# Retention and feed-forward on one core: work moved between places of an instruction order written by hand

## The chip, the core and the metric

The kernel runs on one core of a Trainium2 chip. The metric is the device time of one execution in microseconds (us). Before the change it is 857.37 us, the median of three runs (856.86 to 859.24). Everything below about the kernel before comes from one profiled execution of it. The engines are PE (TensorE matmul), PEld (TensorE weight load), DVE (VectorE), ACT (ScalarE), POOL (GpSimd) and SP (SyncE, which here only issues transfers, DMAs).

## The reference, cut to what matters

Retention (a linear attention with a decay for each head) over 8 batches, 8 heads, 576 positions and 64 channels, and a feed-forward block on its output, all in float32:

```
scores = q @ k.T / 8 ;  ret = scores * gamma_h ** (i - j) for i >= j, else 0
x   = (ret @ v), heads side by side        # 4608 tokens x 512
h   = x @ w_in                             # 512 x 2048
g   = h - tanh(h)
out = g @ w_out                            # 2048 x 512
```

## The kernel before, in words

The 576 positions are cut into nine chunks n = 0 to 8 of 64 positions; a chunk with its 8 batches is a block of 512 tokens. A float32 product is made of three products of rounded words: a tile is split into a high word (an ACT copy that rounds) and a low word (a DVE subtraction), and high by high, high by low and low by high are summed in PSUM. The 2048 middle channels are 16 tiles f of 128, in eight pairs j.

From chunk 3 on two chunks are multiplied with `w_in` at a time by a scheme with seven products in place of eight (`product`, `product_c`; products 0 to 6 of a pair j). It needs seven variants of x (`xv[0]` to `xv[6]`, each a tile of high and one of low words) and seven of each pair of `w_in`, which were written to memory before (`wvar`). What comes out are the four blocks c11, c12, c21 and c22 of h; for each a tanh runs on ACT (L1078, L1277) and a subtraction on POOL (`away`, which also stores g to `spill`) or on DVE (L1105, L1111, L1318).

- `stage_a(3)`: chunks 3 and 4, pairs j = 0 to 7. Chunk 3's g is split into words at once (`split`) and multiplied with `w_out` by `mm2_pair`, one pair behind (L1117); chunk 4's is stored. The block c21 of a pair is finished by `rest` (L1110): for j = 0 it waits in `pending` and runs inside pair 1, for the others it runs at the pair's own end. The sums that make the variants of `w_out` for later are made in `out_sums(j - 1)` (six DVE additions, L1147, two ACT roundings, L1150), called inside pair j behind c22 (L1093); their low words (L1154) and stores follow.
- `stage_b(4, ...)`: chunk 4's g is fetched and multiplied with `w_out` (`mm2`, L572, f = 0 to 15). Before each even f a "stretch" of small 64 x 64 matmuls (L344) computes retention for a later chunk (`stretch`, L935); it reads the running `state`, the masked scores (L356) and v scaled by ACT (`scale_v`, L301, called through `prep_turn(m, 1)`). `out_sums(7)` runs at f = 3, its store at f = 5 (L1528 to L1532).
- `stage_c(5, ...)`: chunks 5 and 6, now with a stretch in front of each of the eight pairs (p = j = 0 to 7). All g goes to `spill`. In the last pair the variants of x are made again for the next stage: `renew(na, k)` is called as soon as product k has been issued (its ACT rounding, L1242), and the low words (L1243) go into the list `lows`, from which `low()` takes one at fixed places.
- `stage_c(7, ...)`: chunks 7 and 8, pairs in falling order (p counts up, j down). It has no stretches; `ahead_c(p, k)` behind product k loads the variants of `w_out` for the second half (`load_second`; the lists `ahead_at` and `SPLITS` say when), splits some of them (`split_second`, L1353 and L1356), fetches the stored g (`fetch_group`) and starts its sums (`side_pieces`).
- The second half multiplies g of chunks 5 to 8 with `w_out` by the same scheme: eight groups of seven products q (`second_product`, L1462 and L1466), in the order `ORDER2` = B11, T1, T2, B22, T3, B21, T4, summed in three PSUM banks by `CHAIN`. In front of each q stand `side(q + 3)` and, for q = 1 to 4, one more `split_second`.

The order of the instructions is that of the program: `in_order` ties each engine's instructions to their order in the code. A buffer is named by its tag, and a tile waits until the one that had its buffer has been read or stored. All loads and stores named here are issued on SP's queue, in program order as well; one that must wait holds up those behind it.

Three buffers take part. The tag "g" has three buffers, which c22, c12 and c21 of every pair share. In `stage_c` the PSUM bank of x (products 0 and 5) is "own" in the last stage and "o0" in the one before, for every pair. The words of `w_out`'s variants go into places that the program has done with: B21's last two tiles into "wo1" and "wo0", which hold words of `w_in` for pair 0, the last to be computed, and the tiles of T3 and T4 into places of `xv`.

Of the kernel before, what the change touches and what calls it, by code (L numbers as in the profile page):

```python
# [19 lines left out]
P = 128  # L20
# [72 lines left out]
def retention_ffn(ctx: ExitStack, tc: tile.TileContext, ins, out, spill, wvar, ovar, ofull):  # L93
# [971 lines left out]
    def stage_a(na):  # L1065

        nb, pending, sums_too = na + 1, [], na + 2 == LATE
        u4 = work[:, 1]
        for j in range(NPAIR):
            u2 = work[:, 3 * (j % 2)]  # L1070
            x, y = [psp.tile([P, BLK], F32, tag=t, bufs=1, name=f"p{t}{na}_{j}") for t in ("new" if j else "o0", "own")]
            z, v = [psp.tile([P, BLK], F32, tag="h", bufs=2, name=f"p{t}{na}_{j}") for t in "zv"]
            f1, f2 = 2 * j, 2 * j + 1
            c22, c12, c21 = [pool.tile([P, BLK], F32, tag="g", bufs=3, name=f"c{t}_{na}_{j}") for t in (22, 12, 21)]

            def tanh(c):
                th = pool.tile([P, BLK], F32, tag="cv", bufs=4, name=f"th{na}_{j}")
                nc.scalar.activation(th, c, AF.Tanh)  # L1078
                return th

            def away(c, f):
                nc.gpsimd.tensor_tensor(c, c, tanh(c), op=ALU.subtract)  # L1082
                nc.sync.dma_start(spill[nb, f], c)

            product(0, x)
            product(1, y)
            nc.scalar.copy(u2, x)
            nc.vector.tensor_tensor(u2, y, u2, op=ALU.add)
            product(2, z)
            nc.vector.tensor_tensor(u4, z, u2, op=ALU.add)  # L1090
            product(3, v)
            nc.vector.tensor_tensor(c22, v, u4, op=ALU.add)
            low_sums = out_sums(j - 1) if sums_too and j > 0 else None  # L1093
            while pending:
                pending.pop()()
            y = psp.tile([P, BLK], F32, tag="own", bufs=1, name=f"py{na}_{j}")
            product(4, y)
            away(c22, f2)
            nc.vector.tensor_tensor(c12, y, u4, op=ALU.add)
            if low_sums:  # L1100
                low_sums()
            product(5, x, False)
            away(c12, f1)
            g11 = tanh(x)
            nc.vector.tensor_tensor(g11, x, g11, op=ALU.subtract)  # L1105
            product(6, v, False)
            split(na, f1, g11, False)
            nc.vector.tensor_tensor(c21, v, u2, op=ALU.add)

            def rest(f=f2, c=c21, tanh=tanh):  # L1110
                nc.vector.tensor_tensor(c, c, tanh(c), op=ALU.subtract)  # L1111
                split(na, f, c, True)

            if j == 0:
                pending.append(rest)
            else:
                mm2_pair(na, j - 1)  # L1117
                rest()
        if sums_too:
            load_turn(held, 1)  # L1120
            load_turn(held + 1, 1)
        for f in range(3):
            fetch(nb, f)
        if sums_too:
            prep_turn(held, 1)
        mm2_pair(na, NPAIR - 1)
        for f in range(2):
            split(nb, f, fetched.pop((nb, f)), False)

    def out_sums(j):  # L1130

        f1, f2 = [wout[2 * j + u].bitcast(F32) for u in range(2)]
        if j == NPAIR - 1:
            both = pool.tile([P, 2, DM], F32, tag="xl0", bufs=1, name=f"r{j}")
            r1, r2 = [both[:, u] for u in range(2)]
            wides = pool.tile([P, 2, 2, 2, Q], F32R, tag="xh0", bufs=1, name=f"to{j}")
            wides = [wides[:, u] for u in range(2)]
        else:
            r1, r2 = [pool.tile([P, DM], F32, tag="cv", bufs=4, name=f"r{j}_{u}") for u in range(2)]
            wides = [pool.tile([P, 2, 2, Q], F32R, tag=t, bufs=1, name=f"to{j}_{t}") for t in ("vr", "one")]  # L1140
        t1, t2, t3, t4 = [w[:, u, 1].bitcast(F32) for w in wides for u in range(2)]
        for to, a, b, op in (
            (r1, f1[:, 0], f1[:, 1], ALU.add), (r2, f2[:, 0], f2[:, 1], ALU.add),
            (t1, r1[:, Q:], r1[:, :Q], ALU.subtract), (t2, r2[:, Q:], t1, ALU.subtract),
            (t3, r2[:, Q:], r1[:, Q:], ALU.subtract), (t4, r2[:, :Q], t2, ALU.subtract),
        ):
            nc.vector.tensor_tensor(to, a, b, op=op)  # L1147
        words = [(T2, wides[0][:, 1:2]), (T3, wides[1])]
        for _, w in words:
            nc.scalar.copy(w[:, :, 0], w[:, :, 1].bitcast(F32))  # L1150

        def low_sums(store=True):
            for _, w in words:
                nc.vector.tensor_tensor(w[:, :, 1], w[:, :, 1].bitcast(F32), w[:, :, 0].bitcast(F32), op=ALU.subtract)  # L1154
            if store:
                store_sums()

        def store_sums():
            nc.sync.dma_start(ofull[:, B11, j], r1[:, :Q])
            nc.sync.dma_start(ofull[:, B21 : B22 + 1, j], r2.rearrange("p (k m) -> p k m", k=2))  # L1160
            nc.sync.dma_start(ofull[:, T1, j], t1)
            for at, w in words:
                n = w.shape[1]
                nc.sync.dma_start(ovar[:, at - T2 : at - T2 + n, j], w.bitcast(F32).rearrange("p v s m -> p v (s m)"))

        return (low_sums, store_sums) if j == NPAIR - 1 else low_sums

    raw, tslots, sources = {}, {}, {}
    RAWS = [(j, v) for j in range(NPAIR) for v in (0, 5, 6)]
# [75 lines left out]
    def stage_c(na, m0, lows):  # L1245

        nb, last_ = na + 1, na + 2 == NC
        if not last_:
            new_sources(na)
        homes_ = ("own", "new", "h", "h") if last_ else ("o0", "o1", "o2", "o3")  # L1250
        for p in range(NPAIR):
            j = NPAIR - 1 - p if last_ else p
            sums_of = None if last_ else attend_c(m0 + j)
            if sums_of and j == NPAIR - 1:
                sums_of()
# [4 lines left out]
                for w, t in zip("xyzv", homes_)  # L1260
            ]
            f1, f2 = 2 * j, 2 * j + 1
            c22, c12, c21 = [pool.tile([P, BLK], F32, tag="g", bufs=3, name=f"c{t}_{na}_{j}") for t in (22, 12, 21)]

            def done(k):
                if last_:
                    ahead_c(p, k)
                elif j == NPAIR - 1:
                    lows.append(renew(na, k))

            def low():
                if lows:
                    lows.pop(0)()
# [9 lines left out]

            product_c(na, j, 0, x)
            nc.scalar.copy(u2, x)
            done(0)
            if not last_:
                load_turn(m0 + j + 3, 0)
# [2 lines left out]
            low()  # L1291
            done(1)
            if not last_:
                prep_turn(m0 + j + 1, 1)
                load_turn(m0 + j + 2, 1)
                load_raws(6 + j)
            product_c(na, j, 2, z)
# [19 lines left out]
            g11 = tanh(x)  # L1317
            nc.vector.tensor_tensor(g11, x, g11, op=ALU.subtract)  # L1318
            nc.sync.dma_start(spill[na, f1], g11)
            low()  # L1320
            done(5)
            product_c(na, j, 6, v, False)
            nc.vector.tensor_tensor(c21, v, u2, op=ALU.add)
            away(na, c21, f2)
            done(6)

    second_w = {}

    def load_second(at, i):

        tags = {
            T1: ["wo12", "wo13", "wo14", "wo15"], B11: ["wo11", "wo10", "wo9", "wo8"],
            B22: ["wo7", "wo6", "wo5", "wo4"], B21: ["wo3", "wo2", "wo1", "wo0"],
        }
        homes_ = [place_of(f) for f in range(NF) if f not in (0, 2)]
        tags |= {T2: [place_of(0), place_of(2), "qk", "qk"], T3: homes_[6:10], T4: homes_[10:14]}
        where, bufs = (pool, 2) if tags[at][i] == "qk" else (const, 1)
        w = where.tile([P, 2, 2, Q], F32R, tag=tags[at][i], bufs=bufs, name=f"w2_{at}_{i}")
        if at < T2:
            nc.sync.dma_start(w[:, :, 1].bitcast(F32), ofull[:, at, 2 * i : 2 * i + 2])  # L1340
            unsplit.append(w)
        else:
            nc.sync.dma_start(w.bitcast(F32).rearrange("p j s m -> p j (s m)"), ovar[:, at - T2, 2 * i : 2 * i + 2])
        for u in range(2):
            second_w[at, 2 * i + u] = w[:, u]
# [15 lines left out]
    def fetch_group(k):  # L1361
# [16 lines left out]
        (0, 0): [(T1, 0), (T1, 1)], (0, 4): [(T1, 2), (T1, 3)], (1, 0): [(B11, 0)], (2, 0): [(B11, 1), (B11, 2)],  # L1378
        (3, 0): [(B11, 3)], (4, 0): [(B22, 0), (B22, 1)], (4, 4): [(T2, 0)], (5, 0): [(B22, 2), (T2, 1)],
        (5, 4): [(T2, 2)], (6, 0): [(B22, 3), (B21, 0)], (6, 4): [(T2, 3)], (7, 0): [(B21, 1)],  # L1380
        (7, 4): [(T3, i) for i in range(4)], (7, 6): [(B21, 2), (B21, 3)],
    }
    SPLITS = [
        (1, 1), (1, 3), (1, 5), (2, 1), (2, 3), (3, 1), (3, 3), (4, 1), (5, 1), (5, 3), (6, 1), (6, 5), (7, 1),
# [123 lines left out]
    def stage_b(n, m0):  # L1508

        fetch(n, 3)  # L1510
        for f in range(NF):
# [14 lines left out]
                load_slot(2)  # L1526
            if n == LATE - 1:
                if f == 3:  # L1528
                    low_sums, store_sums = out_sums(NPAIR - 1)
                    low_sums(False)  # L1530
                if f == 5:
                    store_sums()  # L1532
                if f in (11, 13):
                    load_sums(LATE, (f - 11) // 2)
                if f > 3 and f % 2 == 0:
                    load_raws(f // 2 - 2)
# [125 lines left out]
```

## Time and profile before

| what | value |
|---|---|
| median of three runs | 857.37 us |
| the profiled execution's own time | 857.09 us |
| its span, first to last instruction | 855.3 us |
| PE busy | 829.9 us, 97% of the span |
| DVE, ACT, POOL busy | 70%, 48%, 11% of the span |
| mean granted TensorE clock | 0.993 of full speed |
| transfers | 204.11 MB, 239 GB/s on average |

Where the stages lie, in us from the start of the span: `stage_a(3)` from about 317 to 443, `stage_b(4)` from there to 505, `stage_c(5)` to 602, `stage_c(7)` to 687, the second half from there to the end. PE is busy nearly throughout; the place to read is the little time in which it isn't, and what ended each of those pauses. "Issue" as a releaser means that the profile shows nothing that the engine waited for.

### The profile page before, as it was taken

What the parts mean: (1) busy time and instruction counts of PE and PEld (TensorE: products, weight loads), DVE (VectorE), ACT (ScalarE), POOL (GpSimd) and SP (SyncE); (2) the same over time, 40 slices, a digit from 0 to 9 for tenths busy, and PEclk for the clock granted to TensorE, in tenths of its full rate; (3) what the DMA queues carried; (4) which work ended last, traced back from release to release, by engine and by line L of the source; (5) the groups of instructions that cost most, each with busy time, mean ns of one, the idle gap of its engine ahead of it and who ended that gap; (6) DMA issues with size and microseconds to landing.
All of it is one profiled execution on the core that took longest, in us unless ns stands there. A gap on an engine that the chain in (4) does not pass through costs nothing.

```text
span 855.3 us, 19226 instructions
## 1 busy us (share of the span) xinstructions
PE 829.9 (97%) x7829; PEld 687.0 (80%) x7830; DVE 596.8 (70%) x947; ACT 408.9 (48%) x772; POOL 97.8 (11%) x79
## 2 busy tenths in 40 slices
PE   8999999999999999999989998999899888999997
PEld 6888888888888887888878887888677677888886
DVE  6999877777667665665648665456654768888884
ACT  5987755444245533333244544335443454444542
POOL 0000101010000002111110003233333320000000
PEclk9999999999999999999999999999999999999999
DMA  9968978884777677667378989784579897444411
GB/s 354 360 234 277 346 218 255 243 288 166 229 282 259 206 261 248 227 254 269 137 238 289 328 273 367 257 311 151 196 248 331 284 307 250 152 129 123 123 36 39
DMA packets 94520, 204.11 MB, mean 239 GB/s; under 512 B 9184, under 2 KB 35168, under 8 KB 90976
## 3 DMA queue, kind: packets, MB, share of 16 engines
q1 hardware_dynamic: 93984, 202.10, 69.2%
q8 instruction: 61, 1.00, 0.5%
q10 hardware_dynamic: 448, 0.79, 0.3%
q14 instruction: 27, 0.22, 0.1%
HBM read 135.22 MB, written 67.63 MB: 237 GB/s over the span
## 4 chain that ended last, share of the span: by engine, by line
PE 84%; DMA 5%; issue 4%; DVE 3%; ACT 2%; POOL 1%; SPq 0%; POOLq 0%; DVEq 0%; ACTq 0%
PE o L572 20%; PE h L514 15%; PE b L1462 11%; PE b L1466 6%; PE o L1058 5%; PE px L1195 3%; PE s L344 3%; PE pv L1195 3%; PE new L344 2%; PE pv L1027 2%; PE pnew L1027 2%; PE py L1195 2%; PE pz L1195 2%; PE pw L1195 2%; DMA spill_dram<-c 2%
## 5 line engine op out<-in xcount | busy, mean ns | idle before, releaser
L1462 PE MATMUL b<-w,s 128*128 128x512 f32 x336 | 118.7, 400 | 2.2 <-DVE w L1353 2.2
L572 PE MATMUL o<-wo,gh 128*128 128x512 f32 x432 | 110.8, 394 | 0.2 <-DMA vr<-in_qkv_dram 0.2
L514 PE MATMUL h<-xh,wi 128*128 128x512 f32 x380 | 96.6, 392 | 0.2 <-ACT wi L148 0.2
L572 PEld LDWEIGHTS o<-wo,gh 128*128 128x128 f32 x432 | 79.9, 188 | 18.1 <-DMA vr<-in_qkv_dram 0.6
L1466 PE MATMUL b<-w,s 128*128 128x256 f32 x336 | 87.7, 282 | 0.0
L1281 POOL TENSOR_TENSOR c<-c,th 128x512 f32<-128x512 f32 x48 | 63.4, 1325 | 197.0 <-ACT th L1277 97.7
L514 PEld LDWEIGHTS h<-xh,wi 128*128 128x128 f32 x380 | 70.6, 188 | 15.7 <-ACT wi L148 0.7
L1462 PEld LDWEIGHTS b<-w,s 128*128 128x128 f32 x336 | 61.9, 190 | 14.3 <-DVE w L1353 2.5
L1277 ACT ACTIVATE th<-c 128x512 f32<-128x512 f32 x48 | 30.1, 632 | 85.9 <-DVE c L1306 51.8
L1466 PEld LDWEIGHTS b<-w,s 128*128 128x128 f32 x336 | 64.1, 191 | 3.7
L572 PE MATMUL o<-wo,gl 128*128 128x512 f32 x216 | 59.7, 389 | 0.0
L344 PE MATMUL own<-qk,state 64*64 64x64 f32 x888 | 54.5, 221 | 0.0
L344 PE MATMUL own<-qk,vr 64*64 64x64 f32 x888 | 53.2, 218 | 0.0
L514 PE MATMUL h<-xl,wi 128*128 128x512 f32 x192 | 51.8, 390 | 0.0
L572 PEld LDWEIGHTS o<-wo,gl 128*128 128x128 f32 x216 | 40.5, 188 | 8.4
L1195 PE MATMUL px<-xhv,raw 128*128 128x512 f32 x128 | 41.3, 404 | 4.6 <-DVE th L1318 4.0
L344 PEld LDWEIGHTS own<-qk,vr 64*64 64x64 f32 x888 | 44.4, 135 | 0.0
L344 PEld LDWEIGHTS own<-qk,state 64*64 64x64 f32 x888 | 44.3, 134 | 0.0
L1082 POOL TENSOR_TENSOR c<-c,th 128x512 f32<-128x512 f32 x16 | 21.3, 1345 | 197.4 <-ACT th L1078 184.4
L514 PEld LDWEIGHTS h<-xl,wi 128*128 128x128 f32 x192 | 36.0, 188 | 7.6
L301 ACT ACTIVATE vr<-vr,vtab 128x128 f32<-128x128 f32 x100 | 32.1, 396 | 17.8 <-DMA vr<-in_qkv_dram 17.8
L344 PEld LDWEIGHTS s<-qk 64*64 64x64 f32 x928 | 29.3, 135 | 9.2 <-issue 5.3
(331 smaller groups left out, 1913.1 us busy)
## 6 DMA issues: line engine op xcount, KB each, us to landing
spill_dram<-c SPq DMA_DIRECT2D x64, 256.0 KB, 3.7
s<-spill_dram SPq DMA_DIRECT2D x62, 256.0 KB, 4.0
qk<-in_qkv_dram SPq DMA_DIRECT2D x29, 512.0 KB, 4.8
vr<-in_qkv_dram SPq DMA_DIRECT2D x29, 512.0 KB, 5.0
wt<-wvar_dram SPq DMA_DIRECT2D x14, 1024.0 KB, 6.8
ws<-wvar_dram SPq DMA_DIRECT2D x13, 1024.0 KB, 5.2
spill_dram<-g SPq DMA_DIRECT2D x36, 256.0 KB, 3.5
rwi<-in_w_in_dram SPq DMA_DIRECT2D x16, 512.0 KB, 6.3
```

The source lines that it names most:

```text
L301: nc.scalar.activation(v[:, :, i], v[:, :, i], AF.Copy, scale=vtab[:, n, i : i + 1])
L344: nc.tensor.matmul(out_, w, x, start=start, stop=stop)
L514: nc.tensor.matmul(hp, win[f][:, cc // 2, a, cc % 2 * P : (cc % 2 + 1) * P], x[:, cc, :], start=(k == 0), stop=(k == 3 * NCC - 1))
L572: nc.tensor.matmul(ops[n][t], g[:, t * P : (t + 1) * P], wout[f_][:, a, :], start=(f_ == first and k == 0), stop=(f_ == final and k == 2),)
L1027: nc.tensor.matmul(into, w[:, a, k], x[:, k], start=start and i == 0, stop=i == len(terms) - 1, skip_group_check=not start,)
L1058: nc.tensor.matmul(ops[n][t], g[:, t * P : (t + 1) * P], wout[f][:, a, :], start=(j == 0 and f == fs[0] and k == 0), stop=last_,)
L1082: nc.gpsimd.tensor_tensor(c, c, tanh(c), op=ALU.subtract)
L1195: nc.tensor.matmul(into, w[:, a, k], x[:, k], start=start and i == 0, stop=i == len(terms) - 1, skip_group_check=not start,)
L1277: nc.scalar.activation(th, c, AF.Tanh)
L1281: nc.gpsimd.tensor_tensor(c, c, tanh(c), op=ALU.subtract)
L1462: nc.tensor.matmul(to, hi[:, j], ws, start=fresh and j == 0, stop=last_, skip_group_check=not fresh)
L1466: nc.tensor.matmul(to[:, 0], lo[:, j], ws[:, 0], start=False, stop=False, skip_group_check=not fresh)
```

## The change

In `stage_a` the pending `rest` of pair 0 (c21 minus its tanh, and its words) is issued ahead of `out_sums(0)`. `out_sums(6)` no longer runs inside pair 7: it runs, with its low words, at the stage's very end, in buffers "xh1" and "xl0" rather than in those of v ("vr", "one") and of the "cv" ring, and it is stored at f = 3 of `stage_b(4)`. `out_sums(7)` and its store move from f = 3 and f = 5 to f = 5 and f = 7. The two loads of v for the next stage move from the end of pair 7 to its beginning.

In `stage_c` x's bank alternates between two by the pair ("o0" and "h", in the last stage "o0" and "own"). c21 gets a tile of its own from the tag "gl", so that "g" is shared by two. v's scaling for the next stretch moves from behind product 1 to behind product 5 and x's tanh; the `low()` that stood there goes to the end of the pair, behind c21. `renew(5, 6)` moves from the end of pair 7 into the next stage's first pair, behind the copy of x. B21's last two tiles go into places of `xv[3]` and are loaded at (7, 3) rather than (7, 6); T3 goes into those of `xv[4]` and `xv[5]` and is loaded at (7, 5) rather than (7, 4); T4 goes into those of `xv[6]`, "wo1" and "wo0", still at (7, 6).

```diff
@@ stage_a
+            if sums_too and j == NPAIR - 1:
+                load_turn(held, 1)
+                load_turn(held + 1, 1)
...
-            low_sums = out_sums(j - 1) if sums_too and j > 0 else None
             while pending:
                 pending.pop()()
+            low_sums = out_sums(j - 1) if sums_too and 0 < j < NPAIR - 1 else None
...
-        if sums_too:
-            load_turn(held, 1)
-            load_turn(held + 1, 1)
...
+        if sums_too:
+            stored_sums.append(out_sums(NPAIR - 2))
+            stored_sums[-1][0]()
+
+    stored_sums = []
@@ out_sums
-        if j == NPAIR - 1:
-            both = pool.tile([P, 2, DM], F32, tag="xl0", bufs=1, name=f"r{j}")
+        if j > NPAIR - 3:
+            tags = ("xl0", "xh0") if j == NPAIR - 1 else ("xh1", "xl0")
+            both = pool.tile([P, 2, DM], F32, tag=tags[0], bufs=1, name=f"r{j}")
...
@@ stage_c
-        homes_ = ("own", "new", "h", "h") if last_ else ("o0", "o1", "o2", "o3")
         for p in range(NPAIR):
             j = NPAIR - 1 - p if last_ else p
+            homes_ = (("o0", "own")[p % 2], "new", "h", "h") if last_ else (("o0", "h")[p % 2], "o1", "o2", "o3")
...
-            c22, c12, c21 = [pool.tile([P, BLK], F32, tag="g", bufs=3, name=f"c{t}_{na}_{j}") for t in (22, 12, 21)]
+            c22, c12 = [pool.tile([P, BLK], F32, tag="g", bufs=3, name=f"c{t}_{na}_{j}") for t in (22, 12)]
+            c21 = pool.tile([P, BLK], F32, tag="gl", name=f"c21_{na}_{j}")
...
-                elif j == NPAIR - 1:
+                elif j == NPAIR - 1 and k < 6:
                     lows.append(renew(na, k))
...
             nc.scalar.copy(u2, x)
+            if last_ and p == 0:
+                lows.append(renew(na - 2, 6))
...
-                prep_turn(m0 + j + 1, 1)
                 load_turn(m0 + j + 2, 1)
...
             nc.sync.dma_start(spill[na, f1], g11)
-            low()
+            if not last_:
+                prep_turn(m0 + j + 1, 1)
             done(5)
             product_c(na, j, 6, v, False)
             nc.vector.tensor_tensor(c21, v, u2, op=ALU.add)
             away(na, c21, f2)
+            low()
             done(6)
@@ load_second
-            B22: ["wo7", "wo6", "wo5", "wo4"], B21: ["wo3", "wo2", "wo1", "wo0"],
+            B22: ["wo7", "wo6", "wo5", "wo4"],
...
-        tags |= {T2: [place_of(0), place_of(2), "qk", "qk"], T3: homes_[6:10], T4: homes_[10:14]}
+        tags |= {T2: [place_of(0), place_of(2), "qk", "qk"], T3: homes_[8:12], T4: homes_[12:14] + ["wo1", "wo0"]}
+        tags[B21] = ["wo3", "wo2"] + homes_[6:8]
@@ ahead_at
-        (7, 4): [(T3, i) for i in range(4)], (7, 6): [(B21, 2), (B21, 3)],
+        (7, 3): [(B21, 2), (B21, 3)], (7, 5): [(T3, i) for i in range(4)],
@@ stage_b
             if n == LATE - 1:
                 if f == 3:
+                    stored_sums.pop()[1]()
+                if f == 5:
                     low_sums, store_sums = out_sums(NPAIR - 1)
-                    low_sums(False)
-                if f == 5:
+                    low_sums()
+                if f == 7:
                     store_sums()
```

## Rows read from the trace of the kernel before

**Rows 1.** Page, busy time of PE: us, share of the span, instructions.
```profile
PE 829.9 (97%) x7829; PEld 687.0 (80%) x7830; DVE 596.8 (70%) x947; ACT 408.9 (48%) x772; POOL 97.8 (11%) x79
```
**Rows 2.** What PE waited for, whole span: total us, times, longest us.
```profile
PE o L1058 <- ACT gs L1042: 4.3, 2, 2.4
PE px L1195 <- DVE th L1318: 4.0, 3, 2.1
PE b L1462 <- ACT u L1476: 2.7, 1, 2.7
PE px L1195 <- issue: 2.3, 1, 2.3
PE b L1462 <- DVE w L1353: 2.2, 1, 2.2
...
PE pw L1195 <- DVE ugh L1290: 0.4, 1, 0.4
```
**Rows 3.** Busy us by engine in two stretches, then PEclk, DMA share, GB/s.
```profile
436.60:440.01 3.41, 3.41 (x9) 2.65 (x9) 0.03 (x1) 1.12 (x4) 0.00 (x0) 0.50 0.82 291
535.60:539.00 3.40, 3.40 (x10) 2.62 (x9) 0.69 (x1) 1.57 (x5) 0.00 (x0) 0.50 0.90 337
```
**Rows 4.** Timeline of DVE, 332 to 338: start, us, instruction, idle time before it.
```profile
332.70 1.29 DVE L1147 TENSOR_TENSOR r<-wo 128x512 f32<-128x512 f32 x2
...
336.66 0.69 DVE L1111 TENSOR_TENSOR c<-c,th 128x512 f32<-128x512 f32 x1 [1.22 <-ACT th L1078]
```
**Rows 5.** Timeline of ACT in pair 7 of stage_a.
```profile
430.45 0.60 ACT L1078 ACTIVATE th<-pnew 128x512 f32<-128x512 f32 x1 [1.27 <-POOL c L1082]
```
**Rows 6.** Timeline of DVE and PE at the start of stage_b(4).
```profile
446.05 0.68 DVE L395 TENSOR_TENSOR state<-new,state 128x512 f32<-128x512 f32 x1
451.17 0.27 PE L344 MATMUL own<-qk,state 64*64 64x64 f32 x2
...
459.50 1.28 DVE L1147 TENSOR_TENSOR r<-wo 128x512 f32<-128x512 f32 x2
463.55 0.68 DVE L356 TENSOR_TENSOR qk<-s,mask 128x512 f32<-128x512 f32 x1
```
**Rows 7.** Timeline of ACT and PE in pairs 0 and 1 of stage_c(5).
```profile
515.89 1.28 ACT L301 ACTIVATE vr<-vr,vtab 128x128 f32<-128x128 f32 x4 [6.15 <-DMA vr<-in_qkv_dram]
...
528.48 0.58 ACT L1277 ACTIVATE th<-px 128x512 f32<-128x512 f32 x1
529.40 0.22 PE L344 MATMUL own<-qk,vr 64*64 64x64 f32 x2
529.64 0.23 PE L344 MATMUL own<-qk,vr 64*64 64x64 f32 x2
```
**Rows 8.** Transfers from 531.5 to 534, by queue: packets, MB, share.
```profile
q8 instruction: 1, 0.02, 2.4%
```
**Rows 9.** Timeline of DVE and ACT where stage_c(7) begins.
```profile
603.20 1.34 DVE L1243 TENSOR_TENSOR xlv<-src,xhv 128x1024 fp32r<-128x1024 f32 x1
606.65 0.57 ACT L1285 COPY ugh<-px 128x512 f32<-128x512 f32 x1
```
**Rows 10.** Chain that ended last, two of its pieces: start, us, what.
```profile
654.82 9.46 DMA spill_dram<-c
...
694.35 11.96 DMA go<-spill_dram
```
**Rows 11.** Timeline of SP, ACT and DVE around the second half's first products.
```profile
689.10 0.60 SPq L1319 DMA_DIRECT2D spill_dram<-th  x1
...
699.56 0.62 ACT L1356 CAST w<-w 128x512 fp32r<-128x512 f32 x1 [4.59 <-DMA w<-ofull_dram]
...
706.33 1.23 DVE L1431 TENSOR_TENSOR sums<-ge,go 128x1024 f32<-128x1024 f32 x1 [0.62 <-DMA go<-spill_dram]
707.47 0.68 DVE L1353 TENSOR_TENSOR w<-w 128x512 fp32r<-128x512 f32 x1
```
**Rows 12.** As in rows 3, for the stretch from 694 to 706.3.
```profile
694.00:706.30 12.30, 9.28 (x52) 7.61 (x50) 6.77 (x9) 5.08 (x8) 0.00 (x0) 1.00 1.07 376
```

More of the change, by code (lines that the diff above doesn't have):

```diff
@@ L1128, in stage_a @@
             split(nb, f, fetched.pop((nb, f)), False)
+        if sums_too:
+            stored_sums.append(out_sums(NPAIR - 2))
+            stored_sums[-1][0]()
+    stored_sums = []
     def out_sums(j):
         f1, f2 = [wout[2 * j + u].bitcast(F32) for u in range(2)]
-        if j == NPAIR - 1:
-            both = pool.tile([P, 2, DM], F32, tag="xl0", bufs=1, name=f"r{j}")
+        if j > NPAIR - 3:
+            tags = ("xl0", "xh0") if j == NPAIR - 1 else ("xh1", "xl0")
+            both = pool.tile([P, 2, DM], F32, tag=tags[0], bufs=1, name=f"r{j}")
             r1, r2 = [both[:, u] for u in range(2)]
-            wides = pool.tile([P, 2, 2, 2, Q], F32R, tag="xh0", bufs=1, name=f"to{j}")
+            wides = pool.tile([P, 2, 2, 2, Q], F32R, tag=tags[1], bufs=1, name=f"to{j}")
             wides = [wides[:, u] for u in range(2)]
@@ L1150, in out_sums, with low_sums @@
             nc.scalar.copy(w[:, :, 0], w[:, :, 1].bitcast(F32))
-        def low_sums(store=True):
+        def low_sums():
             for _, w in words:
                 nc.vector.tensor_tensor(w[:, :, 1], w[:, :, 1].bitcast(F32), w[:, :, 0].bitcast(F32), op=ALU.subtract)
-            if store:
+            if j < NPAIR - 2:
                 store_sums()
@@ L1164, in store_sums @@
                 nc.sync.dma_start(ovar[:, at - T2 : at - T2 + n, j], w.bitcast(F32).rearrange("p v s m -> p v (s m)"))
-        return (low_sums, store_sums) if j == NPAIR - 1 else low_sums
+        return (low_sums, store_sums) if j > NPAIR - 3 else low_sums
     raw, tslots, sources = {}, {}, {}
```

## The prediction

> **What bounds the kernel now.** I read the page's busy times first: PE is busy 829.9 us of 855.3 [rows 1], so the time is PE's work plus the little in which it stands still, and another engine counts only where it makes PE wait. The second view is the list of what PE waited for, over the whole span [rows 2]. The reader is to see that five lines hold nearly all of the waiting after the start: 4.3 us in two pieces for the words of g in `stage_a` (2.4 and 1.9), 4.0 in three pieces for x minus its tanh (2.1 the longest; by the gaps in PE's timeline the others are 1.3 and 0.6), 2.7 for a copy on ACT, 2.3 for "issue", 2.2 for a word of `w_out`, and two of 0.4 (one row stands for both). Together 16.3 us. Third, the windows after those pauses [rows 3]: behind three of them (those ending at 435.96, 534.29 and 708.22; two of the three rows stand) the granted clock is 0.50 for 3.4 us, the 1.2 GHz level, and half the clock for 3.4 us is 1.7 us of work. Behind the others it stays at 1.00. A pause that goes may take its 1.7 us along. Last I read each pause in the timelines.
>
> The matmuls are not changed in number or shape, so the change can be worth at most about 16.3 + 3 x 1.7 = 21 us. The sum below goes against the profiled execution's own 857.09 us (span 855.3 and 1.8 around it); the median of the runs shown, 857.37, is 0.3 above that.
>
> **Part by part.** *Words of g in pair 1 of `stage_a`.* DVE starts the six additions of `out_sums(0)` at 332.70, and pair 0's L1111 comes at 336.66 behind them [rows 4]; PE waits for its words until 338.06. Issued first, L1111 can start at about 332.8, as its tanh waits for nothing but ACT's order; 1.4 us later (L1111 0.69, rounding 0.62) the high words are there, at 334.2, and PE wants them at 336.1. The pause of 1.9 goes. What is late next: the sums move back by some 2 us, and with them, through ACT's order, x minus its tanh, which frees x's bank for pair 2. I get 341.4 for that against PE's 341.5. Gain 1.8, between 1.3 and 1.9.
>
> *Pair 7 without `out_sums(6)`.* Here ACT takes x's tanh at 430.45, 1.27 late, since it waits for POOL to give back a buffer of the "cv" ring, two of whose four are held by the sums [rows 5]; the rest of the chain follows to 435.96. Without the sums the tanh can come at 426.8 and the last high words at 432.3; PE comes to them at 433.6. The pause of 2.4 goes, and with it, I expect, the slow stretch behind it [rows 3]: 2.4 + 1.7 = 4.1. Bounds 2.4 and 4.1.
>
> *What that puts into `stage_b(4)`.* The six additions and two low words take DVE from 459.50 to 463.55, 4.05 us, today at f = 3 [rows 6]. At the stage's head they come ahead of the masked scores and of the state's addition at 446.05, which then starts at 450.1 and ends at 450.8; PE reads the state at 451.17 [rows 6]. Cover 0.4 us. ACT's two roundings stand ahead of v's scaling for that stretch, which I find done at 451.1, head by head in time. `out_sums(7)` at f = 5 does the same to the next stretch with about a microsecond to spare; its five stores then stand ahead of a load of v on SP at f = 7, as they did at f = 5, where PE lost 0.2. The earlier loads of v wait for the stores of `out_sums(5)`, with nothing urgent behind them on SP. Cost 0.3, from 0 to 4 if the cover is gone and one set of sums lies on the path.
>
> *v's scaling behind x's tanh in `stage_c(5)`.* In pair 0 ACT stood 6.15 us for a load of v [rows 7], so all of this pair's tanh came late and PE lost 0.6 at the next x; with another bank for x that wait can't recur. Against it: the next stretch wants the scaled v. In pair 1 x's tanh runs from 528.48 to 529.06 and PE reads v at 529.40, the next head at 529.64, 0.24 a head; four scalings take 1.28, 0.29 apart, 0.39 each [rows 7]. The heads would be ready at 529.4, 529.7, 530.0 and 530.3 and are wanted at 529.4, 529.6, 529.9 and 530.1. PE's waits stand once for each head in the trace, so PE loses the difference of the last, 0.2 to 0.3. That is so in pairs 1, 3 and 5, where four additions for x's variants delay c22; in the even ones the tanh is 0.4 us earlier and nothing is lost. Cost 0.8, gain 0.6: 0.2 lost, from 0.6 gained to 3.7 lost.
>
> *Start of the last stage.* A low word of 1.34 us on DVE at 603.20 stands ahead of c21; c21's tanh and the rounding of `xv[6]` follow on ACT, and the copy of x, ready at 603.5, comes at 606.65 [rows 9]. From it hang 0.4, 0.4 and the 1.3 for x [rows 2]. With c21 first, ACT is free at 604.6 and copies x at once; the last low word ends at about 610.7, when PE wants it. x has its second bank. Gain 2.1, between 1.3 and 2.2.
>
> *c21's own buffer.* c22 and c12 of pair 5 waited for stores of the pair before; one took 9.46 us to land, as the fetched g stood ahead of it [rows 10]. Their lateness reached x minus its tanh and PE: 2.1 us. With two tiles in three buffers c22 waits for a store nearly two pairs old, c12 for the last pair's c22, which landed at 662.4, when c12 is wanted; and x no longer stops PE. c21 waits for its predecessor as before, and u4 beside it in "gl" is read long before. Gain 2.1, between 1.0 and 2.1.
>
> *B21 and T3.* ACT stands 4.59 us for B21's third tile, until 699.56, so PE loses 2.7 [rows 2, 11]. Loaded at (7, 3), it travels from 683 in a queue that is nearly empty, and the 2.7 go. The 2.2 at 706 do not go with them. The last low word of B21 (707.47) stands on DVE behind the sum at 706.33, which waits for the `go` of the next group [rows 11], and `go` took 11.96 us from 694.35 [rows 10]. That load keeps its place behind T3, and T3 is issued later: behind the store of 689.10 [rows 11]. Four loads of 512 KB, two stores of 256 KB and `ge` and `go` of 1 MB each are 4.7 MB; at the 376 GB/s of that stretch [rows 12] 12.5 us, with 1 to 2 us until the first lands: `go` at 704.5 in place of 706.3. PE then goes on at 706.4 against 708.22, after a pause of 3.1 us (it would come there at 703.3). Gain 1.8, between 0 and 4.9, and the slow clock behind it stays.
>
> A rule speaks for more. The loads landed in the order of their issue here: those from 686 to 703 all did, `go` after T3 and `ge`. The Trainium skill, "DMA: Bandwidth & Descriptors", section "Queues, rings and completion order", says that completion is not first in, first out for an issuing engine. The trace does not bear that out for loads of this size; by the rule `go` need not wait for T3, which is a rival below.
>
> The sum: -1.8 - 4.1 + 0.3 + 0.2 - 2.1 - 2.1 - 1.8 = -11.4, so 857.1 - 11.4 = **845.7 us**, its own range 842.5 to 849.
>
> **The rivals.** *The pause for "issue" goes as well.* In the 2.3 us before 534.29 PE has all its operands, and one packet of instructions arrives [rows 8]: PE had run out of them behind a stretch of small matmuls. That is the only such pause in some 24 stretches, so a little shift can lift it: 2.3 + 1.7 = 4.0 less, 841.7. Against it: PE's program is nearly the same there. The Trainium skill, "Runtime: NRT & Kernel Launch", section "Instruction fetch mechanics", has the fetch of the next block mostly hidden. By it the pause need not come, 841.7; the trace, with one pause in 24, agrees for the other stretches and not for this one.
>
> *What the last stage gains is given back at q = 5.* If DVE, which has little idle time in pairs 6 and 7, does not come 2.1 us earlier, T3 and `go` don't either, and PE waits longer there: 2.1 + 2.1 less gain, 849.9.
>
> *PE waits for the whole of v.* If a stretch waits for the last of the four scalings, it loses 0.85 in three pairs and 0.45 in four, 4.3 in place of 0.8: 849.2.
>
> *`go` lands ahead of T3.* The pause at 706 goes with its slow stretch: 3.1 + 1.7 = 4.8 less, 840.9.
>
> *Slower: PE runs out of instructions more often.* The pauses gave the fetch time. One such pause costs 4.0 [rows 2, 3]; the forecast turns from the third new one on, at 857.7. For it: the stretches use up their instructions fastest, and the transfer queues are full at that time (337 GB/s, rows 3). Against it: those stretches had no long pause before them in the kernel before either.
>
> **How the numbers follow.** Chances: forecast 0.45, "issue" gone 0.25, given back 0.12, whole of v 0.08, `go` early 0.05, starved 0.05. Range 840.5 to 851.0: it leaves out the slow case and the ends of the others. What a measurement of this kernel can tell from no change is about 0.3%, 2.6 us; below 854.8 lie all cases but the last, and I take off a little for what I haven't seen: faster 0.90, same 0.05, slower 0.05.
>
> **What would show it.** In the list of PE's waits: no line for the words of g, none for x minus its tanh, none for the copy on ACT; a line for the word of `w_out` of about 3 us (none if `go` comes early); new lines of 0.2 to 0.3 for v's scaling, three of them (seven if whole). No 0.50 clock around 436. The additions of `out_sums(6)` on DVE at the head of `stage_b(4)`, and PE's state not waited for. I am wrong if a pause of over 2 us stands where none stood.

## The result and the profile after

The changed kernel takes 845.8 us, median of four runs (844.95 to 850.1); the kernel before, on the same chips, 858.1 (856.86 to 859.24). The ratio is 0.987, with an interval of 0.983 to 0.991. The forecast was 845.7, in a range of 840.5 to 851.0. The profiled execution took 844.95 us (span 843.0), 12.1 less than that of before.

The page's busy times after:

```profile
PE 824.9 (98%) x7829; PEld 687.3 (82%) x7830; DVE 598.0 (71%) x947; ACT 409.3 (49%) x772; POOL 97.9 (12%) x79
```

PE is busy 5.0 us less with the same number of matmuls [rows 1]: less of it ran at half the clock (PE was busy for 7.9 us of the slow stretches, 10.2 before), and 0.4 us a pair was never a pause in the list (below). The other 7 us are pauses. What PE waited for, after:

```profile
PE b L1473 <- DVE w L1364: 4.8, 1, 4.8
...
PE px L1201 <- issue: 1.8, 1, 1.8
...
PE o L572 <- issue: 1.0, 1, 1.0
PE o L572 <- DMA vr<-in_qkv_dram: 0.6, 1, 0.6
PE b L1473 <- ACT u L1487: 0.5, 1, 0.5
```

Against [rows 2], the words of g and x minus its tanh are gone, and so is the 2.7 for the copy on ACT; the 0.5 for it stands at another place (679.98), where there was none before. The word of `w_out` has grown from 2.2 to 4.8. Two lines of 1.0 and 0.6 are new, both in `stage_b(4)`. The granted clock in three stretches after (columns as in [rows 3]):

```profile
437.04:440.45 3.41, 3.41 (x134) 3.12 (x135) 3.38 (x6) 0.43 (x1) 0.00 (x0) 1.00 0.93 195
529.52:532.93 3.41, 3.41 (x10) 2.67 (x9) 0.17 (x1) 0.59 (x1) 0.00 (x0) 0.50 1.01 347
693.36:700.19 6.83, 4.53 (x14) 3.85 (x15) 6.34 (x8) 2.09 (x2) 0.00 (x0) 0.50 1.05 379
```

The reader is to see that no half clock follows the end of `stage_a` any more, that the one behind the pause for instructions is still there, and that the one at the pause of 4.8 lasts 6.83 us in place of 3.4. It begins 2.3 us before that pause ends (695.66), so PE worked for 4.53 us of it.

Where the 12 us came from, by the starts of the first matmul of each stage and pair in PE's timelines of both kernels:

| stretch | forecast | measured |
|---|---|---|
| `stage_a`, to its last product | -1.8 | -1.96 |
| `stage_a`, pair 7 | -4.1 | -4.50 |
| `stage_b(4)` and the start of `stage_c(5)` | +0.3 | +2.03 |
| `stage_c(5)`, pairs and stretches | +0.2 | -0.28 |
| `stage_c(7)`, pair 0 | -2.1 | -3.27 |
| `stage_c(7)`, pairs 1 to 4, 0.41 each | 0 | -1.64 |
| `stage_c(7)`, pair 5 | -2.1 | -2.70 |
| `stage_c(7)`, pairs 6 and 7 | 0 | -0.54 |
| second half of `w_out` | -1.8 | +0.82 |
| sum (PE's end: 850.45 to 838.38, 12.07, of which 0.03 lies ahead of `stage_a`) | -11.4 | -12.04 |

### The profile page after: what moved, and what is told of

It reads as the page before. It is cut to its first block, busy times and chain, and to the rows that moved or that the text cites. A ratio compares the mean times of both kernels' runs of the same rounds, so it can differ in the third digit from the quotient of the medians.

```text
span 843.0 us, 19242 instructions
## 1 busy us (share of the span) xinstructions
PE 824.9 (98%) x7829; PEld 687.3 (82%) x7830; DVE 598.0 (71%) x947; ACT 409.3 (49%) x772; POOL 97.9 (12%) x79
```

## The experiments

**The last wait: DVE's order or the transfers?** PE's pause of 4.8 us ends with the low word of B21. Timelines of ACT, DVE, PE and SP after, around it:

```profile
690.86 1.04 ACT L1432 CAST s<-ge 128x1024 fp32r<-128x1024 f32 x1 [5.56 <-DMA ge<-spill_dram]
...
693.78 1.23 DVE L1442 TENSOR_TENSOR sums<-ge,go 128x1024 f32<-128x1024 f32 x1 [0.61 <-DMA go<-spill_dram]
694.92 0.68 DVE L1364 TENSOR_TENSOR w<-w 128x512 fp32r<-128x512 f32 x1
695.66 0.80 PE L1473 MATMUL b<-w,s 128*128 128x512 f32 x1 [4.80 <-DVE w L1364]
...
676.18 0.33 SPq L1289 DMA_DIRECT2D spill_dram<-c  x1
...
677.08 1.87 SPq L1354 DMA_DIRECT2D w<-ovar_dram  x4
680.98 2.04 SPq L1385 DMA_DIRECT2D go<-spill_dram  x1
```

The word stands behind the sum that wants `go`, as forecast. The last stage's products end at 673.86 after and at 686.76 before; T3 is issued 3.2 us behind the products' end (677.08), and the chain of waits has `go` under way for 12.77 us from 680.98. So `go` lands 19.9 us behind the products' end; before it was 19.6 (694.35 + 11.96, [rows 10]).

*The lower word first*, a cut that leaves the transfers as they are:

```diff
+        if 0 < q < 5:
+            split_second()
         if q + 3 < 7 * len(GROUPS):
             side(q + 3)
-        if 0 < q < 5:
-            split_second()
```

> The kernel after, with the low word of a w_out tile issued ahead of the sums of g in the second half. Theory A (the transfers are late: T3 was issued 3 us after the last stage began to end instead of at once, and all of group 1's g and T4 stand behind it): the 4.8 us in which PE waits for the low word of B21 go, but PE then stands for the tiles of T4, whose four loads landed at 695.0 to 698.9 in the kernel after and are wanted from about 691.6. PE would end T4's product at 698.9 + 0.7 = 699.6 instead of about 701.6: gain 1 to 2.5 us, total 842.5 to 844, with a line 'b <- DMA w' of 3 to 4 us. Rival B (DVE's order alone is the cause: the low word stands behind a sum that waits for go): no wait takes its place, 4.8 us and the 3.4 us of half clock behind it go, total about 837.

Measured: 844.67 us. PE's timeline in this run, at the end of the new pause:

```profile
696.15 0.47 PE L1473 MATMUL b<-w,s 128*128 128x512 f32 x1 [3.91 <-DMA w<-ovar_dram]
```

The word no longer holds PE, and PE stands 3.91 us for T4 instead; the second half is 163.62 us long against 164.52, 0.9 less, a little under the 1 to 2.5 that Theory A gave. DVE's order alone was not the bound. The transfers were.

*Group 1's `go` and `ge` early* (`fetch_group` takes which of the two it loads):

```diff
+        if (p, k) == (7, 0):
+            fetch_group(1, (1,))
+        if (p, k) == (7, 4):
+            fetch_group(1, (0,))
         if (p, k) == (7, 6):
-            fetch_group(1)
             for i in range(4):
                 load_second(T4, i)
```

> The kernel after, with group 1's go fetched in pair 7 behind product 0 and its ge behind product 4, both behind product 6 before. Theory A (queue and bytes): 2 MB less stand between T3 and T4 (5.6 us at 376 GB/s), so go is there before its sum wants it and T4 lands at about 690 to 693.5. The pauses of 4.8 and 0.5 and the slow clock of 6.8 us (3.4 us of work) go: 836.5 to 839, no line for DVE w or DMA w over 1 us in the second half. Rival C (the transfers only change places: what go gains, T3 and B21 lose, with PE standing for them instead): a wait of 3 us or more on w of B21 or T3 in the second half, total 842 to 846. Rival D: the early go cannot start, since its buffer is still in use, and holds up the spill stores behind it on SP: pauses in pairs 6 and 7 of the last stage, total over 845.

Measured: 836.91 us. SP's timeline and PE's waits in this run:

```profile
667.31 0.49 SPq L1385 DMA_DIRECT2D go<-spill_dram  x1
...
672.06 0.39 SPq L1385 DMA_DIRECT2D ge<-spill_dram  x1
```

```profile
PE px L1201 <- issue: 2.0, 1, 2.0
...
PE b L1480 <- DMA w<-ovar_dram: 0.6, 2, 0.3
PE b L1476 <- ACT u L1490: 0.5, 1, 0.5
```

The pause of 4.8 is gone with its slow clock, and only 0.6 us in two pieces takes its place, as by Theory A: the second half is 158.75 us long, 5.8 less than after. That is the gain that the change itself left lying.

*B21's and T3's order alone, in the kernel before* (the change's own lines of `tags` and `ahead_at`, nothing else):

```diff
-        (7, 4): [(T3, i) for i in range(4)], (7, 6): [(B21, 2), (B21, 3)],
+        (7, 3): [(B21, 2), (B21, 3)], (7, 5): [(T3, i) for i in range(4)],
```

> The kernel before, with nothing but the new order and places of the last tiles of B21 and T3. Theory A (what the early B21 gives, the later T3 and go take back: go lands 19 to 20 us after the last stage's products end in either order, and the slow clock behind one long pause lasts longer): PE's 2.7 us wait for the copy on ACT is down to about 0.5, the wait for the low word of B21 grows from 2.2 to 4.5 to 5; from the end of the last stage's products to PE's end 163.7 + 0 to 1.7, total 857 to 859, no gain. Rival B, as forecast (the pause is 3.1 us long, since go lands at 704.5): the second half is 1.8 us shorter, total 855.3.

Measured: 861.27 us, 2 to 4 more than expected, though not through the edit: `stage_a` and `stage_b(4)` of this execution are 1.6 and 2.1 us longer than in the profiled one of before, with the same code. The second half is 163.26 us long against 163.70, so 0.4 gained where I forecast 1.8. Its longest wait:

```profile
PE b L1463 <- DVE w L1354: 4.9, 1, 4.9
```

The copy's 2.7 went, and the word of `w_out` took nearly all of it back.

**x's second bank alone**, in the kernel before:

```diff
-        homes_ = ("own", "new", "h", "h") if last_ else ("o0", "o1", "o2", "o3")
+            homes_ = (("o0", "own")[p % 2], "new", "h", "h") if last_ else (("o0", "h")[p % 2], "o1", "o2", "o3")
```

> The kernel before, with nothing but x's second bank in turn in stage_c. Theory A (the bank accounts for most of what the last stage gained, also the 0.41 us a pair that no listed wait shows): pairs 1 to 5 of the last stage 9.5 us each instead of 9.9, its pauses of 1.3 and 0.4 for x and the 0.6 in stage_c(5) gone, and most of the 2.1 at 665: -2.9 - 1.3 - 0.6 - 2 = about -7 at the last stage's end, total 850 to 853 by what the second half gives back. Rival B (the 0.41 is from c21's buffer or from where the low words stand, not from the bank): pairs stay at 9.9 us, only 1.3 + 0.6 go, total 855. Rival C (the copy of x at 606.65 is what PE waits for, whatever the bank): even the 1.3 stay.

Measured: 860.32 us; the total missed. What this execution lost stands ahead of the edit: 1.0 up to `stage_a`, 1.3 in it and 4.2 in `stage_b(4)`, in code that is the same. Where the edit acts, Theory A holds for the pairs: 9.52 us each in place of 9.93. The timelines show what no list showed. The kernel before, DVE and PE, where a pair of the last stage begins:

```profile
634.18 0.69 DVE L1318 TENSOR_TENSOR th<-px,th 128x512 f32<-128x512 f32 x1 [1.30 <-ACT th L1277]
...
634.20 0.61 PE L1195 MATMUL pv<-xhv,raw 128*128 128x512 f32 x2
634.93 0.73 PE L1195 MATMUL px<-xhv,raw 128*128 128x512 f32 x2
635.50 0.62 PE L1195 MATMUL px<-xlv,raw 128*128 128x512 f32 x2
```

The same place with x's second bank:

```profile
638.51 0.62 PE L1195 MATMUL pv<-xhv,raw 128*128 128x512 f32 x2
638.97 0.62 PE L1195 MATMUL px<-xhv,raw 128*128 128x512 f32 x2
639.42 0.61 PE L1195 MATMUL px<-xlv,raw 128*128 128x512 f32 x2
```

Each of these rows is two matmuls, and the steady step from row to row is 0.45 us. Before, px starts 0.73 behind pv and the next two another 0.57 later, together 0.40 late: PE waited for x minus its tanh (it ends at 634.87) in every pair, but the modelled ends of pv's matmuls cover the pause. With two banks the step is 0.46 and 0.45.

At the start of the stage the bank gives 1.45 of the 3.27: the 1.3 goes, the two of 0.4 stay. That the rest is from the order of the low words is by elimination; that order was not run alone. In pair 5 it gives only 1.19 of the 2.70: c22's sum on DVE, at 666.80, still waits 3.82 us for a store to give back its buffer, and PE then stands for it.

```profile
PE pv L1195 <- DVE c L1306: 1.2, 1, 1.2
```

That c21's own buffer gives the rest fits this wait, but it was not run alone. Pair 6 loses 0.85 here; that is not the buffer's alone, since pair 6 lost 0.7 to 0.8 also in three of the eleven executions in which c21 has its own.

**v's scaling back ahead of product 2**, in the kernel after:

```diff
             if not last_:
+                prep_turn(m0 + j + 1, 1)
                 load_turn(m0 + j + 2, 1)
...
-            if not last_:
-                prep_turn(m0 + j + 1, 1)
             done(5)
```

> The kernel after, with v's scaling in stage_c(5) back ahead of product 2. Theory A (the scaling behind x's tanh costs 0.22 in three pairs and in the last, and x's bank already keeps PE from waiting in pair 0): -0.7 to -0.9 in stage_c(5), pair 0 loses nothing; total about 844.2. Rival B (the place of the scaling is what freed pair 0): pairs 1, 3, 5 and 6 win 0.2 each, but pair 0 loses 0.6 to 0.7 again; total 844.9, no change.

Measured: 842.97 us. Pair 0 loses nothing (0.01), pairs 1, 3 and 5 win 0.22, 0.23 and 0.22 and pair 6 0.25: Theory A, and the forecast price of 0.2 to 0.3 for each. But one pause grew:

```profile
PE px L1201 <- issue: 3.0, 1, 3.0
```

**Is a pause for instructions the kernel's or the execution's?** The kernel after, unchanged, in one more execution:

> The kernel after, unchanged, once more. Theory A (the pauses for instructions and the slow clock behind a pause differ from one execution to the next, in the same kernel): the pauses in stage_b(4) and stage_c(5) for instructions differ from 1.02 and 1.76 us by 0.3 us or more, and the slow clock behind them is there or not; all other landmarks (end of stage_a, pairs of the last stage, the wait of 4.8) agree within 0.2 us. Rival B (they belong to the program's layout): pauses within 0.1 us of those of the first run, slow clock in the same two places.

Measured: 848.25 us, 3.3 more. PE's waits in this execution:

```profile
PE b L1473 <- DVE w L1364: 5.3, 1, 5.3
...
PE o L572 <- DMA vr<-in_qkv_dram: 2.1, 2, 1.2
PE px L1201 <- issue: 2.1, 1, 2.1
...
PE b L1473 <- ACT u L1487: 1.0, 1, 1.0
```

It is neither theory as I put it. The pause in `stage_c(5)` is 0.3 longer and this time without a half clock behind it (1.3 won); the one in `stage_b(4)` is gone, but v is late by 0.9 and 1.2 there; and the rest does not agree within 0.2 either (1.3 lost ahead of `stage_a`, 1.7 in the second half). The lateness of transfers differs by execution, and the pauses with it.

**Fewer transfers ahead of the instructions**, the raw weights two pairs later, in the kernel after ("the page" below is the 16 KB packet of instructions that arrives in the pause):

```diff
-                load_raws(6 + j)
+                for r in ((), (), (6,), (7, 8), (9,), (10,), (11,), ())[j]:
+                    load_raws(r)
```

> The kernel after, with the loads of raw weights (512 KB a pair) left out of pairs 0 and 1 of stage_c(5) and issued in pairs 2 to 6. Theory Q (the page of instructions that ends PE's pause at 526.8 to 528.6 is queued behind the loads: the transfers run at 400 to 426 GB/s from 518 to 526): 1 MB less before it is 2.5 us, so the page comes 1.5 to 2.5 us earlier and the pause of 1.8 to 3.0 us is gone or under 0.5; total about 842 to 843. Rival P (the page is asked for only when PE has used up the one before it): the page still arrives 1 to 1.4 us after PE's stretch ends, the pause stays between 1.5 and 3, total 844 to 846.

Measured: 846.0 us, no gain in total (`stage_b(4)` and the second half of this execution were again slower than in the profiled one of after), and in the pause between the two theories:

```profile
PE px L1201 <- issue: 1.2, 1, 1.2
```

By itself it decides nothing; two more runs below do.

**Three edits at once**, the early group, the early scaling, and the five stores of `out_sums(7)` behind the load of v:

```diff
-                if f == 7:
-                    store_sums()
...
                     load_turn(m + 3 - odd, int(odd), names[6 if odd else 2])
+                if (n, f) == (LATE - 1, 7):
+                    store_sums()
```

> The kernel after, with group 1 of g fetched early, v's scaling back ahead of product 2, and the five stores of out_sums(7) behind the load of v at f = 7 of stage_b(4). Theory A (these three are independent): the second half as in the run with the early group (5.8 us less), stage_c(5) 0.9 less, and the wait of 0.65 us for v at 474.2 goes: 844.95 - 5.8 - 0.9 - 0.65 = 837.6 with the pause for instructions as in the kernel after, 835 without its slow clock. Rival B (the load is late for another reason than the stores ahead of it): the wait for vr at 474 stays at 0.4 to 0.7. Rival C (the stores, issued later, hold up the next loads or PE's later stretch): a new wait of over 0.5 between 475 and 500.

Measured: 844.14 us, 6.5 more than expected. The second half is 159.00 us, as expected; the wait for v at 474 is gone, but there is one of 1.3 at 459, and a pause for instructions of 2.9 in the same stage with a half clock behind it:

```profile
PE o L572 <- issue: 2.9, 1, 2.9
PE px L1201 <- issue: 2.7, 1, 2.7
```

In the executions with the stores where the change put them that pause was 0 to 1.3, so I left this edit out of what follows. Whether the moved stores caused it is not shown: with the stage as before the pause was 0, 1.2 and 1.8 in three executions.

**Four versions, six runs of each.** The early group alone; with the early scaling; with both and the later raw weights; and the early group with the later raw weights. Their edits stand above.

> The kernel after with group 1 of g fetched early alone, timed in five rounds. Theory A (the early group is worth the 5.8 us of the second half in every execution, and the rest of the scatter is the pauses for instructions and the slow clock behind them, 0 to 5 us): median 838 to 839.5, spread of 3 to 6 us, ratio to the kernel before 0.977. Rival B (836.9 was luck with the first part of the program and the second half only trades one wait for another): median over 842.

> The kernel after with the early group and v's scaling back ahead of product 2. Theory S (the early scaling wins 0.9 us in the odd pairs and the last, but the page of instructions then comes later: the pause for it measured 2.3 to 3.0 us in five runs with the early scaling, 1.8 to 2.1 in four with the late one): net 0.2, so median equal to that of the early group alone within 1 us, pause of 2.5 to 3 in stage_c(5). Rival T (the longer pauses are chance): 0.9 us below the early group alone, pause of 1.8 to 2.1.

> As the run before it, with the raw weights of stage_c(5) loaded two pairs later. Theory Q (the page is queued behind loads that were issued 6 to 9 us before it; 512 KB less in each of pairs 0 and 1): pause in stage_c(5) at most 1.8, median 1 us below the one before it and at or below that of the early group alone. Rival P (the page is asked for late, whatever is queued): pause of 2.3 to 3.0, same median.

> The kernel after with the early group and the raw weights two pairs later, v's scaling as in the kernel after. Theory Q: pause for instructions in stage_c(5) 0.8 to 1.5 as in the run with later raws alone (1.24), median 0.7 us below the early group alone. Rival P: pause 1.8 to 2.1, same median.

| version | median (range), us | ratio to before, interval | pause for instructions in `stage_c(5)` |
|---|---|---|---|
| early group | 840.9 (838.6 to 846.0) | 0.981 (0.978 to 0.984) | 2.1 |
| + early scaling | 841.6 (841.1 to 842.5) | 0.980 (0.978 to 0.983) | 2.2 |
| + early scaling, later raw weights | 838.0 (836.9 to 840.9) | 0.977 (0.974 to 0.979) | 1.4 |
| + later raw weights | 839.3 (838.1 to 841.5) | 0.978 (0.975 to 0.980) | 1.2 |

The first median lies 2 us above what I expected: the execution of 836.91 was a lucky one. The second halves are 158.3 to 159.5 us in all four, so the gain of the early group is there every time. On the early scaling Theory S has the time (0.7 more, with overlapping intervals) but not by its reason, since the pause was 2.2 and not 2.5 to 3. Still, over all executions without the later raw weights the pause was 2.2 to 3.0 in the six with the early scaling and 1.8 to 2.1 in the five with the late one; why is open. The later raw weights give 1.6 us at the median behind the late scaling (840.9 to 839.3), where the runs of the two overlap, and 3.7 behind the early one (841.6 to 838.0), where they don't. The latter is more than the 0.8 by which the pause is shorter; how much of it is slow clock that did not come, these runs don't show. The transfers show what goes with it; the window of the pause behind pair 1's stretch, and a little ahead of it, after and in the third version (queue, packets, MB, share of 16 engines):

```profile
q1 hardware_dynamic: 397, 0.99, 97.0%
q8 instruction: 1, 0.02, 2.6%
```

```profile
q1 hardware_dynamic: 335, 0.61, 71.1%
q8 instruction: 1, 0.02, 2.7%
```

The windows are 526.0 to 528.6 and 528.7 to 531.0. The page's one packet of 16 KB takes 1.1 and 1.0 us. What differs is when it starts: counted from the start of the stretch, after 1.5 to 1.6 us in the three executions with the later raw weights and after 1.9 to 3.2 in the eleven without. When PE asked for it no row shows. Over all 14 profiled executions the pause measured 1.2, 1.2 and 1.4 us in the three with the later raw weights and 1.8 to 3.0 in the eleven without: Theory Q, in size about half of what I gave it. The third version is the fastest of all, 21 us under the kernel before (838.0 against 859.0, the median of the 11 runs of it that belong to these).

## Why the prediction was right

The forecast hit the total within 0.1 us of the median, and that is luck: the last stage gained 3.95 us more than its two terms, the second half came out 2.6 worse and `stage_b(4)` 1.7 worse, and these cancelled.

*Right as reasoned.* Both terms of `stage_a`: -1.96 for 1.8, -4.50 for 4.1 (0.4 over its upper bound), and no 0.50 clock behind it. Both pauses stand in the three executions with this stage as before (2.0 and 2.4 us each time) and in none of the eleven with it changed. The cover at the head of `stage_b(4)`: the state's addition starts at 443.53 and ends at 444.21, and PE reads it at 444.98 (forecast: 0.4 us of cover).

```profile
443.53 0.68 DVE L395 TENSOR_TENSOR state<-new,state 128x512 f32<-128x512 f32 x1
...
444.98 0.24 PE L344 MATMUL own<-qk,state 64*64 64x64 f32 x1
```

v's scaling: 0.22 in each of pairs 1, 3 and 5 against 0.2 to 0.3, and the 0.6 of pair 0 came back as 0.69. I had pair 6 at nothing; it lost 0.25. The run with the scaling back shows that the 0.69 is the bank's. No line for the scaling stands in the list of PE's waits, where I had expected three; the steps show it. Without the shorter pause for instructions (0.54) `stage_c(5)` lost 0.3, for 0.2 forecast.

*Mis-sized: the start of the last stage, x's bank and c21's buffer.* The prediction counted x minus its tanh by the list of waits, "4.0 in three pieces". The same wait was also in pairs 1 to 4 and 6, 0.41 each, where the list has no line for it, and pair 0 held more than its listed pauses: -3.27 for 2.1. So the 21 us that I called the most was not a ceiling. The whole stage gained 8.15 us for 4.2 forecast; the run with the bank alone shows the 0.41.

*Wrong in sign: B21 and T3.* The step that failed is "`go` at 704.5 in place of 706.3" with "a pause of 3.1 us". I had T3 issued 2.3 us behind the last products' end and 15.4 us from there to `go` (0.9 more than the 12.5 and 1 to 2 us that I gave for it). It was 3.2 and 16.7 (677.08 to 693.75); from 678 to 692 the transfers ran at 342 GB/s, where I had taken 376. PE went on 21.8 us behind the products' end and not 19.6: that is 2.2 of the 2.6 us missed. The slow clock, which I had let stay, cost some 0.5 more than before.

The 16.7 comes without the rest of the change too: in the run with B21's and T3's order alone T3 is issued 2.5 us behind the products' end, `go` lands 16.7 us later, and PE goes on at 21.1. Of the 0.9 us by which T3 came late 0.7 go back to DVE. The products ended 12.9 us earlier than before, but the sum for c22 in pair 7 came only 12.2 earlier (DVE before, then after):

```profile
683.10 0.68 DVE L1306 TENSOR_TENSOR c<-pv,ugl 128x512 f32<-128x512 f32 x1
...
670.94 0.68 DVE L1314 TENSOR_TENSOR c<-pv,ugl 128x512 f32<-128x512 f32 x1
```

Behind it the tanh on ACT and the subtractions on POOL stand 0.7 to 0.8 us later against PE, and SP came to T3 only behind a store that waited for POOL (676.18 above). ACT's copy of the first product's bank is as late, and that is the new pause of 0.5.

The loads again landed in the order of their issue: T3's four at 681.3 to 687.1, `go` at 693.8, T4's four at 695.0 to 698.9, so the rival by which `go` comes early is out. The Trainium skill, "DMA: Bandwidth & Descriptors", section "Queues, rings and completion order", has completion not first in, first out. This trace does not show it for these loads.

*Mis-sized by the execution, not by the change: `stage_b(4)`.* It came out at +2.03 for +0.3, mostly through the 0.65 for v and the 1.0 for instructions. From its first matmul to the first product of `stage_c(5)` the stage took 64.0, 68.2 and 66.1 us in three executions with the code of before, and 65.0 to 68.1 in ten with the code of after; the means are 66.1 and 66.2. The profiled execution of before was the shortest of all. So the change cost this stage nothing that these runs can tell, and the 2 us between the two profiled executions lie within the scatter.

*The rivals.* The pause for "issue" stayed (1.8 for 2.3). "Given back at q = 5" happened, in part for its own reason: DVE gained 0.7 us less than PE and made T3 late, but the larger part of the longer pause is the slower transfers. PE did not wait for the whole of v. Of the starved case one new pause of 1.0 was seen, one of those that come and go.

## What to carry to other kernels

A wait that is shorter than the modelled end of the last matmul stands in no list of waits; compare the step from group to group with the steady step inside a group, over every repetition. Before an in-order wait is moved on its engine, look at when the data of the next wait lands: moving the word gave 0.9 us, and fetching 2 MB some 6 and 11 us earlier (against the end of the products) gave 5.8. And a term of under 2 us is not read from one profiled execution of each kernel: take the stage's length over several.

## What the runs showed of the hardware

*The half clock is not a fixed price of a pause.* The same pause of 2.0 us in `stage_a` (to 338.06 before) was followed by a granted clock of 1.00 in the profiled execution of before, and by 0.5 for some 3.4 us in the two runs with the same code there. In the run with x's bank alone (0.5 is the 1.2 GHz level):

```profile
340.00:343.20 3.20, 3.20 (x9) 2.55 (x8) 2.52 (x5) 1.73 (x3) 2.63 (x2) 0.51 0.45 158
```

Of the eleven pauses of 1.8 to 3.0 us for instructions in `stage_c(5)`, six had a half clock behind them, the 1.8 among these, and five had none, the 3.0 among these; behind the three of 1.2 to 1.4 there was none. So in "2.4 + 1.7" the 1.7 has a chance and no fixed size: behind the 2.4 the half clock came in all three executions that have this pause, and the term measured 4.5. Nor does the length of the slow stretch follow that of the pause: of five pauses of 4.8 to 5.3 us for the word of `w_out` it lasted 6.8 us at four and 3.4 at one (the 4.9).

*Instructions.* Each of the 14 pauses in `stage_c(5)` ended 1.2 to 1.6 us after a 16 KB packet of the instruction queue did (after: 526.01 + 1.10, PE goes on at 528.57). The Trainium skill, "Runtime: NRT & Kernel Launch", section "Instruction fetch mechanics", has an engine fetch its next page while it works on the one it has, mostly hidden. Here it did not hold for the page behind pair 1's stretch of small matmuls, in any of 14 executions; the transfers ran at 386 GB/s there after.
